# Two heads in one score product: half-zero query columns, loads by four heads, seven experts side by side

## The chip, the cores and the metric

The kernel runs on one core of a Trainium2 chip. The metric is the device time of one execution in microseconds (us), lower is better. Before the change it is 274.84 us, the median of three runs (272.33, 274.84 and 274.95).

The core has five engines that run their own queues of instructions: TensorE (PE, matrix products and transposes; PEld is its loading of stationary operands), VectorE (DVE), ScalarE (ACT), GpSimd (POOL) and SyncE (SP). Products are written to the memory PSUM, and DVE or ACT move them on to SBUF. POOL and SP also start DMA transfers.

## The reference

```python
def _attn_ref(q, k, v):                       # q, k, v: (8, 8, 576, 64)
    scores = np.matmul(q, k.transpose(0, 1, 3, 2)) / np.sqrt(64)
    rel = pos[:, None] - pos[None, :]
    scores = np.where((rel >= 0) & (rel < 64), scores, -1e9)
    ...softmax over the last axis...
    return np.matmul(attn, v)

def _moe_ref(x, phi, w1, w2):                 # x: (4608, 512), phi: (512, 32)
    logits = x @ phi
    d = softmax of logits over the tokens     # 8 experts x 4 slots = 32 columns
    slot_input = (d.T @ x).reshape(8, 4, 512)
    for e in range(8):                        # w1: (8, 512, 1024), w2: (8, 1024, 512)
        slot_out[e] = np.maximum(slot_input[e] @ w1[e], 0) @ w2[e]
    c = softmax of logits over the slots
    return c @ slot_out                       # (4608, 512)
```

First attention with a causal window of 64 keys, for 8 batches of 8 heads; its output, heads side by side, is x. Then a soft mixture of experts: 32 slots take a weighted mean over all tokens, each expert works on its four slots, and every token gets a weighted mean of the slots' results.

## The kernel before

**Stages.** First a loop over 32 pairs of heads (a batch has four pairs), staggered: in step n different pairs are in different stages. Then, once all batches are through, the slots' softmax is closed, the experts run, and the result is combined and written out (the last 63 us of the profile).

**A step n of the loop** issues in this order, as written out by hand (`manual_schedule`); each engine executes its own part in that order:

- `st_transpose` of pair n: 36 transposes of 64x64 blocks of q and k into tile tp (line 232).
- `st_score` of pair n-3: first ten products that write mask and maximum as a bias (`lh` with `rt`, lines 270 and 274), then 18 products of a block of 64 queries with 128 keys (lines 278 and 283). The two heads of a pair lie in partitions 0 to 63 and 64 to 127, so each product has 64 rows.
- `st_copy` of pair n: ACT brings the transposes of q and k to SBUF (line 235).
- `st_exp` of pair n-3: ACT, the exponentials of the scores (lines 291 and 292).
- `st_av` of pair n-4: 20 products of weights with values (lines 305 and 307). v1 holds v in blocks of 128 tokens, v2 the same shifted by 64.
- `st_shift` of pair n-2: transposes the maxima of the blocks of queries (line 258), DVE casts them into `rt` (line 262).
- `st_norm` of pair n-4: DVE divides by the sums and writes x_b (lines 316 and 317).
- `st_max` of pair n-1: two mask products of 480 columns (line 243), 36 products of 32 queries with 96 keys (line 250), and DVE's maximum over the keys (line 253).
- `fr_transpose` of pair n-5: five transposes of x (line 331), copied by ACT (line 332).
- Every fourth step one part of the mixture's softmax over tokens: logits (line 339, then DVE and the exponentials d of lines 355 to 358), dispatch (lines 386 to 392), the sums over tokens (lines 399 to 411).

The maximum that goes into the bias must not be below the largest score of a block, so scores are made twice: once for the maximum, once for the exponentials.

**Buffers.** The loop has four PSUM tiles of two banks that the names tp, sc, av, mx and f take in turn. Writes and reads of a tile are ordered by semaphores. `pin` holds two buffers each of q and k, a batch in each; POOL issues every load of q, k, v and weights (lines 76, 102, 104, 154), and copies v1 to v2 (lines 158 and 159).

**Experts.** Experts 0 to 3 run side by side: their products write 32 partitions each (lines 541 to 561). Experts 4 to 7 run one after another: 32 products of 4 columns (line 570), ReLU on ACT (line 573), eight products of 512 columns (line 578).

Of the kernel before, what the change touches and what calls it, by code (L numbers as in the profile page):

```python
# [18 lines left out]
def kernel(  # L19
# [33 lines left out]
    pin = ctx.enter_context(tc.tile_pool(name="pin", bufs=2))  # L53
# [5 lines left out]

    RQ = 9  # L60
    assert S == 64 * RQ

    def flat(src, b):
        return src[b].rearrange("h s d -> (h s) d").rearrange("(c p) d -> p c d", p=128)

    def rows(src, b):
        return src[b].rearrange("h s d -> (h s d)").rearrange("(g p x) -> p g x", p=128, x=RQ * Dh)

    staged = {}

    def new_qk(b):
        staged[b] = tuple(pin.tile([128, HP, RQ * Dh], FP16, name=n, tag=n) for n in ("qs", "ks"))

    def load_qk(b, c0=0, c1=HP):
        for t_, src in zip(staged[b], (q, k)):
            nc.gpsimd.dma_start(out=t_[:, c0:c1, :], in_=rows(src, b)[:, c0:c1, :])

    new_qk(0)
    load_qk(0, 0, 1)

    ident_h = const.tile([128, 128], FP16, name="ident_h")
    make_identity(nc, ident_h)
    load_qk(0, 1, HP)
# [22 lines left out]
    def load_last():  # L106
        e = E - 1
        w1_t[e], w2_t[e] = [], []
        for i in range(2):
            a = pin.tile([128, 2, F], FP16, name="w1h", tag="qs")  # L110
            nc.gpsimd.dma_start(out=a, in_=w1_dram(e)[:, 2 * i:2 * i + 2, :])
            w1_t[e].extend(a[:, j, :] for j in range(2))
        for i in range(2):
            c = pin.tile([128, 4, D], FP16, name="w2h", tag="ks")
            for j0, j1 in ((0, 4),) if i == 0 else ((0, 2), (2, 4)):
                nc.gpsimd.dma_start(out=c[:, j0:j1, :], in_=w2_dram(e)[:, 4 * i + j0:4 * i + j1, :])
            w2_t[e].extend(c[:, j, :] for j in range(4))


    wb = const.tile([32, 96], FP16, name="wb")  # L120
    nc.vector.memset(wb, 0.0)
    nc.gpsimd.affine_select(out=wb, in_=wb, compare_op=ALU.is_gt, fill=NEG,
                            base=0, pattern=[[1, 96]], channel_multiplier=-1)
    nc.gpsimd.affine_select(out=wb, in_=wb, compare_op=ALU.is_ge, fill=NEG,
                            base=64, pattern=[[-1, 96]], channel_multiplier=1)

    KR = 75
    mb = const.tile([64, 128], FP16, name="mb")
    nc.vector.memset(mb, 0.0)
    nc.gpsimd.affine_select(out=mb[:, 0:64], in_=mb[:, 0:64], compare_op=ALU.is_gt,  # L130
                            fill=NEG, base=0, pattern=[[1, 64]], channel_multiplier=-1)
    nc.gpsimd.affine_select(out=mb[:, 64:128], in_=mb[:, 64:128], compare_op=ALU.is_ge,
                            fill=NEG, base=0, pattern=[[-1, 64]], channel_multiplier=1)
    db = const.tile([128, 12], FP16, name="db")
    nc.vector.memset(db[64:128, :], 0.0)
    nc.gpsimd.affine_select(out=db[64:KR, 0:10], in_=db[64:KR, 0:10], compare_op=ALU.not_equal, fill=-1.0,
                            base=0, pattern=[[-1, 10]], channel_multiplier=1)
    nc.gpsimd.affine_select(out=db[64:KR, 10:11], in_=db[64:KR, 10:11], compare_op=ALU.not_equal, fill=NEG,
                            base=-10, pattern=[[0, 1]], channel_multiplier=1)
    nc.gpsimd.affine_select(out=db[64:KR, 11:12], in_=db[64:KR, 11:12], compare_op=ALU.not_equal, fill=1.0,  # L140
                            base=-10, pattern=[[0, 1]], channel_multiplier=1)
# [9 lines left out]
    v2s = [pvv.tile([128, NCH, VP], FP16, name=f"v2_{i}") for i in range(2)]  # L151

    def load_v(b):
        nc.gpsimd.dma_start(out=v1s[b % 2][:, :, 0:Dh], in_=flat(v, b))  # L154

    def shift_v(b):
        v1, v2 = v1s[b % 2], v2s[b % 2]
        nc.gpsimd.tensor_copy(out=v2[64:128, :, 0:Dh], in_=v1[0:64, :, 0:Dh])  # L158
        nc.gpsimd.tensor_copy(out=v2[0:64, 1:NCH, 0:Dh], in_=v1[64:128, 0:NCH - 1, 0:Dh])  # L159

    load_v(0)
    new_qk(1)
    load_qk(1)

    NQ = 4
    qkT = [pqk.tile([128, 2, 64 + S], FP16, name=f"qkT{i}") for i in range(NQ)]
    for t_ in qkT:
        nc.vector.memset(t_[:, 1, 0:64], 0.0)
    wm = const.tile([128, 5, 96], FP16, name="wm")
    for t in range(4):  # L170
        nc.vector.tensor_copy(out=wm[32 * t:32 * t + 32],
                              in_=wb[:, :].unsqueeze(1).broadcast_to([32, 5, 96]))
    nc.vector.memset(wm[0:32, 0, 0:64], NEG)
    nc.vector.memset(wm[32:64, 0, 0:32], NEG)

    lh = const.tile([128, 10, 128], FP16, name="lh")
    nc.vector.tensor_copy(out=lh[0:64], in_=mb[:, :].unsqueeze(1).broadcast_to([64, 10, 128]))
    nc.vector.tensor_copy(out=lh[64:128], in_=db[64:128, 0:10].unsqueeze(2).broadcast_to([64, 10, 128]))
    for u in (0, 5):
        nc.vector.tensor_tensor(out=lh[64:128, u, 0:64], in0=lh[64:128, u, 0:64],  # L180
                                in1=db[64:128, 10:11].broadcast_to([64, 64]), op=ALU.add)
    NR = 3
    rts = [const.tile([128, 128], FP16, name=f"rt{i}") for i in range(NR)]
    for rt in rts:
        nc.vector.memset(rt[64:128, 64:128], 0.0)
        nc.vector.tensor_copy(out=rt[64:128, 0:64], in_=db[64:128, 11:12].broadcast_to([64, 64]))
        nc.vector.tensor_copy(out=rt[0:64, 0:64], in_=ident_h[0:64, 0:64])
        nc.vector.tensor_copy(out=rt[0:64, 64:128], in_=ident_h[0:64, 0:64])
# [37 lines left out]
    def st_transpose(p, tq):  # L226
        b, hp = divmod(p, HP)
        for w, src in enumerate(staged[b]):
            for r in range(RQ):
                for hl in range(2):  # L230
                    h = slice(64 * hl, 64 * hl + 64)
                    nc.tensor.transpose(tq[h, w, 64 * r:64 * r + 64], src[h, hp, Dh * r:Dh * r + Dh], ident_h[h, h])  # L232

    def st_copy(p, tq):
        nc.scalar.activation(qkT[p % NQ][:, :, 64:64 + S].rearrange("p w (g r) -> p w g r", r=RQ),  # L235
                             tq[:, :, 0:S].rearrange("p w (r g) -> p w g r", r=RQ), AF.Copy, scale=QKS)

    def st_max(p):
        qk = qkT[p % NQ]
        m = pw.tile([128, 10], FP16, name="m", tag="m")  # L240
        mx, _ = banks("mx")
        for hl in range(2):
            nc.tensor.matmul(mx[:, hl, 0:480], ident_h[:, :], wm[:, :, :].rearrange("p c x -> p (c x)"),  # L243
                             start=True, stop=False, skip_group_check=True)
        for c in range(5):
            for t in range(4 if c < 4 else 2):
                o = 32 * (4 * c + t)
                for hl in range(2):
                    r = slice(64 * hl, 64 * hl + 64)
                    nc.tensor.matmul(mx[32 * t:32 * t + 32, hl, 96 * c:96 * c + 96],  # L250
                                     qk[r, 0, 64 + o:64 + o + 32], qk[r, 1, o:o + 96],
                                     start=False, stop=True, skip_group_check=True)
        nc.vector.reduce_max(m[:, :].rearrange("p (l c) -> p l c", l=2),  # L253
                             mx[:, :, 0:480].rearrange("p l (c x) -> p l c x", x=96), axis=AXX)
        mts[p] = m

    def st_shift(p, av):
        nc.tensor.matmul(av[64:74, 1, 384:512], mts.pop(p)[:, :], ident_h[:, :], start=True, stop=True,  # L258
                         skip_group_check=True)

    def st_shift_copy(p, av):
        nc.vector.tensor_copy(out=rts[p % NR][64:74, :], in_=av[64:74, 1, 384:512])  # L262

    def st_score(p, tp):
        qk, rt = qkT[p % NQ], rts[p % NR]
        pt = pw.tile([128, 2, 9, 64], FP16, name="pt", tag="pt")
        sc, _ = banks("sc")
        sm = tp[:, :, 288:352]
        for hl in range(2):
            nc.tensor.matmul(sm[:, hl, :], lh[:, 5 * hl + 4, :], rt[:, 0:64],  # L270
                             start=True, stop=False, skip_group_check=True)
        for hl in range(2):
            for c in range(4):
                nc.tensor.matmul(sc[:, hl, 128 * c:128 * c + 128], lh[:, 5 * hl + c, :], rt[:, :],  # L274
                                 start=(c == 0), stop=False, skip_group_check=True)
        for hl in range(2):
            r = slice(64 * hl, 64 * hl + 64)
            nc.tensor.matmul(sm[:, hl, :], qk[r, 1, 512:640], qk[r, 0, 576:640],  # L278
                             start=False, stop=True, skip_group_check=True)
# [30 lines left out]
    def st_norm(p, av):  # L310
        b, hp = divmod(p, HP)
        if hp == 0:
            xbs[b] = pxb.tile([128, 5, D], FP16, name="x_b", tag="x_b")
# [109 lines left out]
    for n in range(NP + 8):  # L423
# [7 lines left out]
        if ph == 3 and kb < B:  # L431
            shift_v(kb)
# [207 lines left out]
```

## Time and profile before

| | |
|---|---|
| time, median of 3 runs | 274.84 us |
| profiled execution: time | 271.76 us |
| its span, first to last instruction | 270.0 us |
| mean granted TensorE clock | 0.80 of full speed |
| steps 3 to 31 of the loop, scores' end to scores' end | 19.44 to 180.11 us |
| last slot product of the loop | 206.2 us |
| experts (line 541 to the copies so4) | 213.4 to 238.7 us |
| DMA, mean rate | 152 GB/s |

The profile is of one execution, somewhat below the median; sums are made against it. "Busy" is the share of time in which an engine executes an instruction. A busy TensorE need not run at its peak: products overlap, and its clock, which the profile gives as granted, is at times half. The chain of work that ended last can be followed back in this profile only to 207 us, so the loop is read from its timeline and from the waits.

### The profile page before, as it was taken

What the parts mean: (1) busy time and instruction counts of PE and PEld (TensorE: products, weight loads), DVE (VectorE), ACT (ScalarE), POOL (GpSimd) and SP (SyncE); (2) the same over time, 40 slices, a digit from 0 to 9 for tenths busy, and PEclk for the clock granted to TensorE, in tenths of its full rate; (3) what the DMA queues carried; (4) which work ended last, traced back from release to release, by engine and by line L of the source; (5) the groups of instructions that cost most, each with busy time, mean ns of one, the idle gap of its engine ahead of it and who ended that gap; (6) DMA issues with size and microseconds to landing.
All of it is one profiled execution on the core that took longest, in us unless ns stands there. A gap on an engine that the chain in (4) does not pass through costs nothing. (4 is left out here: it accounts for less than half of the span.)

```text
span 270.0 us, 9905 instructions
## 1 busy us (share of the span) xinstructions
PE 185.6 (69%) x4563; PEld 122.6 (45%) x4563; DVE 140.9 (52%) x313; ACT 120.5 (45%) x215; POOL 78.0 (29%) x74
## 2 busy tenths in 40 slices
PE   2386858858868897887887586878663488866400
PEld 1254646646646665665665365555531134521100
DVE  2743563674754576674485554656664621056510
ACT  2235445655455475574654647462632111155400
POOL 8566064342370533443057033740000000000000
PEclk9998989986985897997799689975955557995555
DMA  6999997992999599199299959899960000029996
GB/s 84 175 206 210 181 208 131 177 207 38 132 211 208 58 187 206 17 177 208 37 100 210 210 73 184 121 203 205 210 105 0 0 4 0 2 101 344 359 359 234
DMA packets 63625, 41.06 MB, mean 152 GB/s; under 512 B 38496, under 2 KB 54880, under 8 KB 63584
## 3 DMA queue, kind: packets, MB, share of 16 engines
q0 software_dynamic: 58064, 30.94, 84.3%
q1 hardware_dynamic: 5520, 9.50, 10.2%
q8 instruction: 35, 0.57, 0.8%
q14 instruction: 6, 0.05, 0.1%
HBM read 61.93 MB, written 9.44 MB: 264 GB/s over the span
## 5 line engine op out<-in xcount | busy, mean ns | idle before, releaser
L235 ACT ACTIVATE qkT<-tp 128x1152 f16<-128x1152 f16 x32 | 36.2, 1131 | 50.2 <-PE tp L278 39.6
L253 DVE TENSOR_REDUCE m<-mx 128x10 f16<-128x960 f32 x32 | 36.8, 1150 | 6.4 <-PE mx L250 6.2
L262 DVE CAST rt<-av 10x128 f16<-10x128 f32 x32 | 9.2, 289 | 51.6 <-PE av L258 50.9
L292 ACT ACTIVATE pt<-sc 128x1024 f16<-128x1024 f32 x32 | 32.9, 1029 | 0.6 <-PE sc L283 0.5
L332 ACT COPY xt<-f 128x576 f16<-128x576 f16 x32 | 20.5, 640 | 26.5 <-PE f L331 26.5
L154 POOL DMA_DIRECT2D v<-in_v_dram x8 | 14.6, 1823 | 55.3 <-issue 35.2
L158 POOL COPY v<-v 64x2304 f16<-64x2304 f16 x8 | 16.8, 2102 | 41.6 <-DMA v<-in_v_dram 41.6
L317 DVE TENSOR_TENSOR x_b<-av,rc 128x640 f16<-128x640 f32 x32 | 26.4, 824 | 1.1
L305 PE MATMUL av<-v,pt 128*64 128x65 f16 x576 | 19.7, 214 | 8.0 <-issue 8.0
L232 PE MATMUL tp<-ident_h,qs 64*64 64x64 f16 x576 | 17.6, 210 | 11.0 <-DMA qs<-in_q_dram 7.9
L274 PE MATMUL sc<-rt,lh 128*128 128x128 f16 x256 | 23.9, 247 | 1.4 <-issue 1.4
L243 PE MATMUL mx<-wm,ident_h 128*128 128x480 f16 x64 | 21.7, 426 | 3.0 <-ACT pt L291 2.7
L305 PEld LDWEIGHTS <-pt 128*64 128x64 f16 x576 | 15.3, 125 | 12.2 <-issue 8.6
L232 PEld LDWEIGHTS <-qs 64*64 64x64 f16 x576 | 14.2, 122 | 14.4 <-DMA qs<-in_q_dram 8.0
L232 PE MATMUL tp<-ident_h,ks 64*64 64x64 f16 x576 | 17.6, 210 | 4.6 <-issue 2.4
L250 PEld LDWEIGHTS <-qkT 64*32 64x32 f16 x1152 | 11.3, 97 | 18.5 <-issue 18.3
L274 PEld LDWEIGHTS <-lh 128*128 128x128 f16 x256 | 18.4, 113 | 1.6 <-issue 1.6
L283 PE MATMUL sc<-qkT 64*128 64x64 f16 x512 | 15.8, 205 | 4.4 <-issue 4.4
L331 PE MATMUL f<-ident_h,x_b 128*128 128x128 f16 x160 | 16.3, 240 | 2.5 <-ACT pt L291 1.2
L250 PE MATMUL mx<-qkT 64*32 64x96 f16 x1152 | 16.2, 221 | 2.2 <-issue 2.2
L232 PEld LDWEIGHTS <-ks 64*64 64x64 f16 x576 | 14.6, 125 | 5.1 <-DMA ks<-in_k_dram 2.6
L159 POOL COPY v<-v 64x2240 f16<-64x2240 f16 x8 | 16.4, 2052 | 0.5
(135 smaller groups left out, 295.0 us busy)
## 6 DMA issues: line engine op xcount, KB each, us to landing
w<-in_moe_w_dram POOLq DMA_DIRECT2D x14, 1024.0 KB, 15.6
out_dram<-ob SPq DMA_DIRECT2D x16, 512.0 KB, 4.5
v<-in_v_dram POOLq DMA_DIRECT2D x8, 576.0 KB, 8.4
qs<-in_q_dram POOLq DMA_DIRECT2D x7, 576.0 KB, 9.6
ks<-in_k_dram POOLq DMA_DIRECT2D x7, 576.0 KB, 11.6
w1h<-in_moe_w_dram POOLq DMA_DIRECT2D x2, 512.0 KB, 18.6
out_dram<-ob SPq DMA_DIRECT2D x8, 128.0 KB, 4.5
w2h<-in_moe_w_dram POOLq DMA_DIRECT2D x1, 512.0 KB, 19.1
```

Of the source, the lines that this page charges most:

```text
L158: nc.gpsimd.tensor_copy(out=v2[64:128, :, 0:Dh], in_=v1[0:64, :, 0:Dh])
L159: nc.gpsimd.tensor_copy(out=v2[0:64, 1:NCH, 0:Dh], in_=v1[64:128, 0:NCH - 1, 0:Dh])
L232: nc.tensor.transpose(tq[h, w, 64 * r:64 * r + 64], src[h, hp, Dh * r:Dh * r + Dh], ident_h[h, h])
L235: nc.scalar.activation(qkT[p % NQ][:, :, 64:64 + S].rearrange("p w (g r) -> p w g r", r=RQ), tq[:, :, 0:S].rearrange("p w (r g) -> p w g r ...
L243: nc.tensor.matmul(mx[:, hl, 0:480], ident_h[:, :], wm[:, :, :].rearrange("p c x -> p (c x)"), start=True, stop=False, skip_group_check=True)
L250: nc.tensor.matmul(mx[32 * t:32 * t + 32, hl, 96 * c:96 * c + 96], qk[r, 0, 64 + o:64 + o + 32], qk[r, 1, o:o + 96], start=False, stop=Tru ...
L253: nc.vector.reduce_max(m[:, :].rearrange("p (l c) -> p l c", l=2), mx[:, :, 0:480].rearrange("p l (c x) -> p l c x", x=96), axis=AXX)
L274: nc.tensor.matmul(sc[:, hl, 128 * c:128 * c + 128], lh[:, 5 * hl + c, :], rt[:, :], start=(c == 0), stop=False, skip_group_check=True)
L292: nc.scalar.activation(pt[:, :, 0:8, :].rearrange("p l i x -> p l (i x)"), sc[:, :, :], AF.Exp, scale=XS)
L305: nc.tensor.matmul(av[r0:r0 + 64, hl, 65 * (i // 2):65 * (i // 2) + 65], pt[:, hl, i, :], rhs, start=True, stop=True, skip_group_check=True)
L317: nc.vector.tensor_tensor(out=xbs[b][:, :, 128 * hp:128 * hp + 128].rearrange("p c (l d) -> p l c d", l=2), in0=avv[:, :, :, 0:64], in1=rc ...
L332: nc.scalar.copy(out=xts[b][:, hp, :], in_=fq[:, 0, 0:S])
```

## The change

In the loop the two heads of a score product now stand in one product of 128 rows. Four heads are loaded together (`load_rows`: a "quad", a step of two loads of 288 KB for k and q, one for v). Even steps transpose k of a quad, odd steps q. After the transpose the partitions hold 64 dimensions of head h and 64 of head h+2; q goes into `qbs`, where each block has 64 columns for the first head with zeros in the lower partitions and 64 columns for the second with zeros in the upper ones. One product of 128x128 then gives the scores of both heads.

- `st_transpose`: 18 transposes a step instead of 36, of 128 rows. `st_copy`: one activation for k, two for q.
- `st_max` of pair n-2 in place of n-1: 3 mask products and 9 products of 128x128 instead of 2 and 36; the ninth block's place is in tile tp (`m8`), and DVE's maximum is split in two.
- `st_shift` moves to pair n-3, in the same step as its score, and writes to tile tp instead of av.
- `st_score`: 9 bias and 9 score products instead of 10 and 18; its ninth block's place is in av instead of tp.
- The order in a step: transposes, copy, shift with its cast, maximum, scores with exponentials, values, normalising.
- `fr_transpose`: ten transposes and one copy every second step instead of five and one every step.
- Loads of q, k and v by quads, four buffers; v2 is shifted by quads; v is loaded two steps earlier. The weights' loads stand at steps 0, 3, 6 to 30.
- Experts 4, 5 and 6 run side by side as a second group; only expert 7 goes by itself.

```diff
-    pin = ctx.enter_context(tc.tile_pool(name="pin", bufs=2))
+    pin = ctx.enter_context(tc.tile_pool(name="pin", bufs=4))
...
+    def load_rows(src, g, tag):
+        t = pin.tile([128, 2, RQ * Dh], FP16, name=tag, tag=tag)
+        b, gq = divmod(g, 2)
+        nc.gpsimd.dma_start(out=t, in_=src[b].rearrange("h s d -> (h s d)").rearrange(
+            "(g p x) -> p g x", p=128, x=RQ * Dh)[:, 2 * gq:2 * gq + 2, :])
+        staged[tag, g] = t
...
+    def load_v(g):
+        b, gq = divmod(g, 2)
+        c = slice(NVC * gq, NVC * gq + NVC)
+        nc.gpsimd.dma_start(out=v1s[b % 2][:, c, 0:Dh],
+                            in_=v[b].rearrange("h s d -> (h s) d").rearrange("(c p) d -> p c d", p=128)[:, c, :])
...
+    def st_transpose(n, tq):
+        g, odd = divmod(n, 2)
+        src = staged.pop(("qs" if odd else "ks", g))
+        tf = tq.rearrange("p a x -> p (a x)")
+        for r in range(RQ):
+            for hf in range(2):
+                nc.tensor.transpose(tf[64 * hf:64 * hf + 64, 128 * r:128 * r + 128],
+                                    src[:, hf, Dh * r:Dh * r + Dh], ident_h[:, :])
+
+    def st_copy(n, tq):
+        g, odd = divmod(n, 2)
+        tf = tq.rearrange("p a x -> p (a x)")[:, 0:2 * S].rearrange("p (r l g) -> p l g r", r=RQ, l=2)
+        if odd:
+            for hf in range(2):
+                h = slice(64 * hf, 64 * hf + 64)
+                nc.scalar.activation(qbs[g % 2][h, :, :, hf, :], tf[h], AF.Copy, scale=QKS)
+        else:
+            nc.scalar.activation(kTs[g % NK][:, :, 64:64 + S], tf, AF.Copy, scale=QKS)
...
+    def at(two, one, i):
+        return two[:, i // 4, 128 * (i % 4):128 * (i % 4) + 128] if i < 8 else one
...
+        m8 = tp[:, 1, 256:384]
+        nc.tensor.matmul(m8, ident_h[:, :], wm[:, 1, :], start=True, stop=False, skip_group_check=True)
+        for j in range(2):
+            nc.tensor.matmul(mx[:, j, :], ident_h[:, :], wm[:, j:j + 4, :].rearrange("p c x -> p (c x)"),
                              start=True, stop=False, skip_group_check=True)
...
+        for i in [8] + list(range(8)):
+            nc.tensor.matmul(at(mx, m8, i), qblock(p, i), kwindow(p, i), start=False, stop=True,
+                             skip_group_check=True)
+        nc.vector.reduce_max(m[:, 8:9], m8, axis=AXX)
...
+        nc.tensor.matmul(tp[64:64 + NB, 1, 128:256], mts.pop(p)[:, 0:NB], ident_h[:, :], start=True, stop=True,
                          skip_group_check=True)
...
+        nc.vector.tensor_copy(out=rts[p % NR][64:64 + NB, :], in_=tp[64:64 + NB, 1, 128:256])
...
+        sm = av[:, 0, 384:512]
+        order = [8] + list(range(8))
+        for i in order:
+            nc.tensor.matmul(at(sc, sm, i), lh[:, i, :], rt[:, :], start=(i % 4 == 0), stop=False,
+                             skip_group_check=True)
+        for i in order:
+            nc.tensor.matmul(at(sc, sm, i), kwindow(p, i), qblock(p, i), start=False, stop=True,
+                             skip_group_check=True)
...
         if n < NP:
             st_transpose(n, tq)
+            st_copy(n, tq)
         if 0 <= n - 3 < NP:
-            sc, sm = st_score(n - 3, tp)
...
+            st_shift(n - 3, tp)
+        if 0 <= n - 2 < NP:
+            st_max(n - 2, tp)
+        if 0 <= n - 3 < NP or 0 <= n - 4 < NP:
             av, _ = banks("av")
+        if 0 <= n - 3 < NP:
+            st_score(n - 3, av)
         if 0 <= n - 4 < NP:
             st_av(n - 4, av)
...
+    groups = ((0, 1, 2, 3), (4, 5, 6))
...
+    for g, es in enumerate(groups):
+        ha, _ = banks("ha")
+        n = 32 * len(es)
+        for f2 in range(2):
+            for kk in range(NKK):
+                for j, e in enumerate(es):
+                    nc.tensor.matmul(ha[32 * j:32 * j + 32, f2, :], sit[:, kk, :],
+                                     w1_t[e][kk][:, 512 * f2:512 * f2 + 512],
+                                     start=(kk == 0), stop=(kk == NKK - 1), skip_group_check=True)
```

## The prediction

> **What bounds the kernel now.** I read the page first. No engine is full: TensorE (PE) is busy 69% of the span. The granted clock changes between full and half; and the program's own instructions come by DMA in 35 packets (0.57 MB, so 16 KB each; PE's 2 x 4563 rows are about 260 a packet).
>
> ```profile
> PE 185.6 (69%) x4563; PEld 122.6 (45%) x4563; DVE 140.9 (52%) x313; ACT 120.5 (45%) x215; POOL 78.0 (29%) x74
> ...
> PEclk9998989986985897997799689975955557995555
> ...
> q8 instruction: 35, 0.57, 0.8%
> ```
>
> Then the timeline of one undisturbed step of the loop (start, duration, instruction; the bracket is idle time and what ended it). The step before began its transposes at 113.67 and this one at 117.48, as soon as the large exponential had ended: 3.81 us a step, made of transposes, bias and score products (1.5 us of PE) and then on ScalarE (ACT) the copy of the transposes, 1.13, and two exponentials, 0.27 and 1.03. While ACT copies, PE does weighted values, shift and maximum products: they belong to other pairs and wait for nothing new.
>
> ```profile
> 116.40 1.03 ACT L292 ACTIVATE pt<-sc 128x1024 f16<-128x1024 f32 x1
> 117.48 0.47 PE L232 MATMUL tp<-ident_h,qs 64*64 64x64 f16 x18 [0.19 <-ACT pt L292]
> ...
> 118.24 0.61 PE L274 MATMUL sc<-rt,lh 128*128 128x128 f16 x8
> 118.82 0.40 PE L283 MATMUL sc<-qkT 64*128 64x64 f16 x16
> 119.03 1.13 ACT L235 ACTIVATE qkT<-tp 128x1152 f16<-128x1152 f16 x1 [1.05 <-PE tp L278]
> 119.58 0.22 PE L258 MATMUL av<-ident_h,m 128*10 128x128 f16 x1
> 119.84 0.29 DVE L262 CAST rt<-av 10x128 f16<-10x128 f32 x1 [1.35 <-PE av L258]
> 120.21 1.03 ACT L292 ACTIVATE pt<-sc 128x1024 f16<-128x1024 f32 x1
> 120.25 0.47 PE L250 MATMUL mx<-qkT 64*32 64x96 f16 x36
> ```
>
> The list of waits (total, times, longest) says two more things. L399 writes one bank of tile f while ACT reads the other, and still waits: a wait goes by whole tile. And PE stands at "issue", with nothing of the program in the way, every 256 rows or so: 14 such gaps of 0.8 to 2.7 us between 20 and 180 us, 24 us in all, each near one of the instruction packets.
>
> ```profile
> ACT qkT L235 <- PE tp L278: 39.6, 24, 3.3
> PE av L305 <- issue: 8.0, 5, 2.7
> PE f L399 <- ACT xt L332: 5.1, 7, 0.7
> ```
>
> Last, busy time in windows as long as the clock's stretches (multiples of 3.41 us). 57% busy at full clock was followed by full clock, 51% by half; half ended only after a window with PE busy throughout.
>
> ```profile
> 164.63:168.04 3.41, 1.95 (x78) 1.67 (x76) 0.89 (x1) 2.36 (x4) 1.69 (x1) 1.00 1.49 204
> 168.04:171.45 3.41, 2.62 (x98) 1.79 (x99) 2.08 (x4) 0.57 (x2) 3.35 (x4) 1.00 0.81 153
> 174.87:178.29 3.42, 1.74 (x53) 1.42 (x50) 2.85 (x6) 2.85 (x7) 0.17 (x1) 1.00 1.18 194
> 178.29:181.70 3.41, 3.06 (x49) 1.79 (x46) 0.60 (x3) 2.21 (x3) 2.70 (x4) 0.50 1.15 211
> ```
>
> The score products of step 3 end at 19.44 and those of step 31 at 180.11: 28 steps of 5.74 us, the 3.81 plus instruction gaps, half clock and the softmax over slots that comes every fourth step. That is 161 of 270 us and where the change acts.
>
> **What it does to a step.** PE's order in the changed program is: 18 transposes, shift, 1+2 mask products, 9 maximum products, 9 bias, 9 scores, 20 weighted values, then transposes of x (10, every second step). Tile tp is now written by the transposes, read by the copy, written by the shift, read by VectorE's (DVE) cast, and written by the maximum's ninth block. So by the whole-tile rule PE stops after the transposes until the copy ends, stops again for the cast, and all the products that the copy used to cover stand behind these two waits. The built program has both waits. The copy in turn queues on ACT behind the large exponential of the step before. The loop becomes one chain, each link from a row above, hops of 0.05 included:
> - after the last score (S): exponential 1.08;
> - even steps: copy of x, now 128x1152 once in two steps. It has the size of L235, 1.13, less 0.1 of overlap; PE's transposes end first (S+0.95);
> - copy of transposes: k in one of 1.13; q in two, each on 64 partitions, each with all 1152 elements a partition. No such row is shown. ACT took 266 ns for 128x128 and 178 for 64x32, 0.9 ns an element whatever the partitions, so 2 x 1.13, overlapped 2.2. (If half the partitions cost half: 1.1, and 15 us less in the whole; I keep that for the lower end.)
> - shift to end of cast: 119.58 to 120.13, 0.6 with hops;
> - products to the new S: 0.06 + 2 x 0.21 (L243, 0.2 for 480 columns) + 27 at 57 ns (L274: 8 in 0.61, of which 0.2 is latency) + 0.2 = 2.2.
>
> Even to odd: 1.08+1.02+2.2+0.6+2.2 = 7.1. Odd to even: 1.08+1.13+0.05+0.6+2.2 = 5.05. Two steps 12.15, against 7.6 for two undisturbed ones now. Weighted values (0.5), transposes (0.7: 128x64 tiles in two column halves like L305; one by one like L274 it would be 1.2, of which 0.3 would show in even steps) and the maximum's reduce (1.22 for 1024 elements by L253) lie beside the exponential and cost nothing; were that cover gone, transposes and values would add 1.2 a step.
>
> Every fourth step adds the slots' work in the same queues. Logits: the d exponentials wait for DVE (normalise to S+1.4, then 1.5 of reductions) and take 1.2; the next copy is behind them: +3.0. Dispatch: +1.2 (PE waits for the copy of x, then two copies and an exponential on ACT). Accumulation: +0.95 (slot products, and DVE's combine ahead of the cast). From step 3 to 31: 14 x 12.15 = 170, and 6 x 3.0 + 6 x 1.2 + 5 x 0.95 = 30. **200 us against 161: +39**, at full clock.
>
> **Clock.** Of 7 us PE is busy some 4.1 (0.7+0.2+2.2+0.5+0.3+0.2), 57%, and the idle part is in one piece of 1.2 to 4 us before the long run of products. The window that holds it falls under the 51-57% seen above, so the products start at half clock, until a window lies inside the run. They have 2.0 us of streaming, which half clock doubles: 0 to 2.0 more a step. I take 0.6 of it, since the run (at half: 4.2 plus values, transposes) holds one full window and often regains full clock at its end: 1.2 x 28 = **+33**.
>
> **Fewer products.** 74 a pair instead of 128, but not less PE time: 16 L283 take 0.2 us beside latency, the nine that replace them 0.5; 36 L250 take 0.25, their nine 0.5. By the Trainium skill ("TensorE: Matmul & The Clock Gate", section Back-to-back issue gap) starts lie at least 25 ns apart however small the product, and 54 fewer would save 1.35 us a step, 43 us in all. The trace disagrees: 36 in 0.47 us, 7 ns apart. What does go is instruction gaps: 5534 PE rows for 9118, and 256 rows now last about 12 us where the packets came every 5 to 6. The chain was summed without them; were all 13 left, +20.
>
> **Loads and v.** Loads of 288 KB start earlier and smaller; PE waited for q and k only in the first 12 us (8 us). Step 3's scores come about 3 us earlier (maxima after the second k, near 10.5): **-3**. The tenth value product reads chunk 0 of v1, which the load for two batches later is now writing in step 4b-2: that load is issued when the previous step's values end and is needed a step (8 us) later. 576 KB landed in 8.4 us, 144 KB in 3.3: 0, bounded by 6 x 1.5 = 9. It holds POOL's queue, where k, q, weights and shifts stand with several steps to spare. Constants: beside the first loads.
>
> **Drain and experts.** After the last score the lags (9, 10, 11) are the same: 26 us now, +-1 either way; I add 1. Experts: from 213.4 to 238.7 now. Three of four rounds of L570/L573/L578 go (3.05 each, 9.2, and 1.2 of L578 at half clock). Added: two more halves of L541 (1.9 each at half clock, less some), 24 more of L557 (1.7 to 2.4). 10.4-3.6-2 = 4.8, and the copy osb is halved over two engines and partly covered: **-6** (-3 to -8).
>
> **Sum.** Profiled execution 271.76 (span 270.0): +39+33-3+1-6 = 336. The median of the runs shown is 274.84, 1.1% above it: 339.
>
> **Rivals.**
> - *The chain at full clock.* If only a stretch without any product slowed the clock, no idle piece here (up to 4 us, never a whole window) would, and the second term is 0: 303, or 306 on the median. Against it: 174.87, halved at 51% busy. The Trainium skill says this ("TensorE: Matmul & The Clock Gate", Part 1 and the table at its end): an idle window of about 3.4 us throttles, gaps under 3 us do not. The trace has half clock after windows that were half busy. 15%.
> - *Half clock nearly always:* 2.0 plus 0.4 for transposes that then delay the copy, x 28 = 67: 370, 374 on the median. For it: 178.29 stayed half at 3.06 of 3.41 busy. 13%.
> - *Faster: PE's feed is the bound.* If the copy and cast wait is covered after all, the 24 us of instruction gaps go and -3-6 stay: 271.8-33 = 239. It decides where the new serial part costs under 24/28 = 0.86 us a step. Against: copy plus cast alone are 1.7 to 2.8, and the tile wait is in the rows of L399. 5%.
> - *Partly covered* (q copies cheaper, extras hidden): 275 to 300, 5%.
>
> **Numbers.** Main case 62%: 339, its own range 315 to 362. Range 300 to 365: it takes in the full-clock case and leaves out the faster ones and most of the always-half one. 1% is what a measurement tells from no change: faster 0.05, same 0.01, slower 0.94.
>
> **What would show it.** The shift's line waiting on ACT's copy 1 us or more in nearly every step; the ninth block's line on DVE's cast; transposes 5 to 9 us apart, long after even steps; q's copy twice 1.13; PEclk near 0.7 in the loop; "issue" gone from PE. Wrong if PE does not idle between transposes and shift, or if steps stay under 6 us.

## The result, and the profile after

The changed kernel takes 359.32 us (median of four runs, 357.96 to 360.36); the kernel before takes 273.58 (median of four, 269.22 to 274.95). The ratio is 1.327, with a 95% interval of 1.312 to 1.342: 86 us slower. The profiled execution after took 360.36 us, its span is 358.6 against 270.0. Some executions of a kernel run over 1.5% longer than its fastest, and one of e1_untie took 761.6 us with TensorE slow from end to end: the medians below are over all executions but that one, the ratios and their intervals without any of the slow ones.

The page of the kernel after, in the rows that were shown of the one before, and one group of instructions:

```profile
PE 215.3 (60%) x2771; PEld 159.9 (45%) x2771; DVE 155.9 (43%) x341; ACT 142.4 (40%) x214; POOL 96.4 (27%) x113
...
PEclk9999869866886679886788666668987885579555
...
q8 instruction: 21, 0.34, 0.4%
...
L248 ACT ACTIVATE qb<-tp 64x1152 f16<-64x1152 f16 x32 | 36.0, 1125 | 4.9 <-PE tp L239 4.5
```

PE has 1792 products fewer and is nevertheless busy 30 us longer; more of its time is at half clock (mean granted clock 0.767 against 0.799). 14 of the 35 instruction packets are gone. The copy of q on 64 partitions takes 1125 ns, as long as the old one on 128 (1131).

The timeline shows what a step has become. In the row of 174.66 the bracket says that PE sat idle for 2.74 us and that ACT's copy ended it.

```profile
171.22 0.69 PE L239 MATMUL tp<-ident_h,qs 128*64 128x128 f16 x18
171.33 1.12 ACT L339 COPY xt<-f 128x1152 f16<-128x1152 f16 x1 [0.68 <-PE f L337]
...
172.35 2.26 ACT L248 ACTIVATE qb<-tp 64x1152 f16<-64x1152 f16 x2
174.66 0.27 PE L278 MATMUL tp<-ident_h,m 128*9 128x128 f16 x1 [2.74 <-ACT qb L248]
...
174.96 0.29 DVE L280 CAST rt<-tp 9x128 f16<-9x128 f32 x1 [3.48 <-PE tp L278]
175.30 0.26 PE L265 MATMUL tp<-wm,ident_h 128*128 128x128 f16 x1 [0.38 <-DVE rt L280]
...
176.32 1.06 PE L270 MATMUL mx<-kT,qb 128*128 128x128 f16 x8
...
177.28 0.86 PE L289 MATMUL sc<-rt,lh 128*128 128x128 f16 x8
...
178.04 0.61 PE L292 MATMUL sc<-qb,kT 128*128 128x128 f16 x8
...
178.30 0.28 ACT L294 ACTIVATE pt<-av 128x128 f16<-128x128 f32 x1 [3.69 <-PE av L292]
```

The engines take turns: transposes, copy of x, copy of q, shift, cast, then 30 products, of which the first eight of L270 take 1.06 us at half clock and the eight of L292 0.61 at full; ACT meanwhile has nothing to do for 3.69 us. Before, the copy had products of other pairs beside it.

The list of waits (total, times, longest) has the same three links over the whole execution:

```profile
PE tp L278 <- ACT qb L248: 38.1, 15, 2.7
...
PE tp L278 <- ACT kT L250: 31.7, 14, 4.0
...
PE tp L265 <- DVE rt L280: 18.3, 31, 2.7
```

Together PE stands 88 us behind the copy and the cast, two waits that the kernel before did not have. PE's own waits for "issue", 22 us in 17 pieces before, are gone from the list.

Where the 88.6 us of span are:

| stretch | before | after | difference |
|---|---|---|---|
| up to the scores of step 3 | 19.4 | 22.4 | +2.9 |
| steps 3 to 31, scores' end to scores' end | 160.7 | 251.2 | +90.5 |
| from there to the last slot product | 26.1 | 30.3 | +4.2 |
| to the first expert product | 7.2 | 7.2 | 0 |
| experts, to the copies so4 | 25.3 | 17.0 | -8.3 |
| combine and write out | 31.3 | 30.5 | -0.8 |

### The profile page after: what moved, and what is told of

It is laid out like the page before. It is cut to its first block, busy times and chain, and to the rows that moved or that the text cites. A ratio compares the mean times of both kernels' runs of the same rounds, so it can differ in the third digit from the quotient of the medians.

```text
span 358.6 us, 6470 instructions
## 1 busy us (share of the span) xinstructions
PE 215.3 (60%) x2771; PEld 159.9 (45%) x2771; DVE 155.9 (43%) x341; ACT 142.4 (40%) x214; POOL 96.4 (27%) x113
## 5 line engine op out<-in xcount | busy, mean ns | idle before, releaser
L273 DVE TENSOR_REDUCE m<-mx 128x8 f16<-128x1024 f32 x32 | 39.2, 1225 | 15.4 <-PE mx L270 15.2
L248 ACT ACTIVATE qb<-tp 64x1152 f16<-64x1152 f16 x32 | 36.0, 1125 | 4.9 <-PE tp L239 4.5
L270 PEld LDWEIGHTS <-qb 128*128 128x128 f16 x288 | 30.5, 139 | 14.8 <-issue 12.7
L270 PE MATMUL mx<-kT,qb 128*128 128x128 f16 x256 | 31.2, 295 | 0.0
L292 PE MATMUL sc<-qb,kT 128*128 128x128 f16 x256 | 29.5, 284 | 0.0
L267 PE MATMUL mx<-wm,ident_h 128*128 128x512 f16 x64 | 29.4, 556 | 0.0
L292 PEld LDWEIGHTS <-kT 128*128 128x128 f16 x288 | 28.2, 136 | 0.0
L71 POOL DMA_DIRECT2D qs<-in_q_dram x16 | 11.4, 712 | 52.2 <-PE tp L239 51.5
L321 DVE RECIPROCAL rc<-av 128x10 f32<-128x10 f32 x32 | 7.1, 221 | 39.4 <-PE av L311 39.4
L250 ACT ACTIVATE kT<-tp 128x1152 f16<-128x1152 f16 x16 | 18.1, 1131 | 9.9 <-PE tp L239 9.6
L339 ACT COPY xt<-f 128x1152 f16<-128x1152 f16 x16 | 17.9, 1119 | 10.0 <-PE f L337 9.0
```

Source lines behind the costliest of these rows:

```text
L248: nc.scalar.activation(qbs[g % 2][h, :, :, hf, :], tf[h], AF.Copy, scale=QKS)
L250: nc.scalar.activation(kTs[g % NK][:, :, 64:64 + S], tf, AF.Copy, scale=QKS)
L267: nc.tensor.matmul(mx[:, j, :], ident_h[:, :], wm[:, j:j + 4, :].rearrange("p c x -> p (c x)"), start=True, stop=False, skip_group_check=True)
L270: nc.tensor.matmul(at(mx, m8, i), qblock(p, i), kwindow(p, i), start=False, stop=True, skip_group_check=True)
L273: nc.vector.reduce_max(m[:, 0:8].rearrange("p (l c) -> p l c", l=2), mx[:, :, :].rearrange("p l (c x) -> p l c x", x=128), axis=AXX)
L292: nc.tensor.matmul(at(sc, sm, i), kwindow(p, i), qblock(p, i), start=False, stop=True, skip_group_check=True)
```

## The experiments

Theory: the change turned the loop into one chain, because by the whole-tile rule shift and maxima, and with them everything behind them in PE's queue, wait for the copy of the same step (the tile tie); the idle piece that this makes drops the clock. Rivals: the wide products or the longer copies are themselves the loss; the clock is lost for another reason; loads are late.

**Untying the tiles.** In e1b_shift the shift alone leaves tile tp, for tile f, and goes ahead of the transposes; in e1_untie and e1_again the ninth block of the maxima also leaves tp, for av.

```diff
-    def st_shift(p, tp):
-        nc.tensor.matmul(tp[64:64 + NB, 1, 128:256], ...
+    def st_shift(p, f, bank):
+        nc.tensor.matmul(f[64:64 + NB, bank, 384:512], ...
...
-        m8 = tp[:, 1, 256:384]
+        m8 = av[:, 1, 384:512]          # e1_untie, e1_again
...
+            st_shift(n - 3, f, 0 if sb is not None else 1)
             st_transpose(n, tq)
             st_copy(n, tq)
-            st_shift(n - 3, tp)
```

> The changed kernel with the shift alone moved to tile f; the maximum's ninth block stays in tile tp behind the copy. Chain theory: the copy still stands in the chain, only shift and cast (20.9 us in 28 steps, 0.6 to 1.9 each) go out of it: 17 to 21 us less, 338 to 343. Rival, the two waits are one and the same and the copy alone decides: no change, 356 to 361. Rival, the shift was the tie that mattered: as fast as with both moved, below 300.

> The changed kernel with the shift moved to tile f and the maximum's ninth block to tile av, so that nothing behind the transposes on TensorE waits for ScalarE's copy of the same step; all products, copies and exponentials stay. Chain theory: the step is then set by ScalarE (7.1 us in two steps and about 1 us a step of the slots' work) or by TensorE alone (about 4.4 us at full clock), 4.8 to 5.8 us a step instead of 8.97, so 28 steps give 89 to 117 us back: 242 to 270 us, and TensorE no longer idles between transposes and mask products. Rival, the wide products themselves at half clock are the cost (3.6 us of products, 0.5 of values, 0.7 of transposes and 0.7 of the rest a step): 6 us a step or more, 275 to 300. Rival, ScalarE's longer copies are the cost whatever TensorE waits for: above 330.

> The changed kernel with the shift in tile f and the ninth block of the maxima in tile av, so that nothing behind the transposes waits for their copy: the kernel of e1_untie once more, to see what bounds it, since the profiled execution of the first was not like the timed ones. Its timed median was 295, 6.6 us a step from 295-359 = -64 us in 28 steps against 8.97. Theory 1, the clock: PE works 5 us a step at mixed clock and the products (27 of 128 columns before the scores, 9+9 after) run at half rate in most steps; then products that come in eights take 0.9 to 1.1 us, and the granted clock is near 0.8. Theory 2, a wait that took the place of the removed one: PE idles before one line in nearly every step, by 1 us or more, for ACT or DVE; then the list of waits has one pair with 28 or more times and over 28 us in all. Time 293 to 297 by both.

e1b_shift: 337.54 us, just under the chain's 338 to 343. e1_untie: 293.63, ratio to before 1.091 (1.081 to 1.101): 64 us of the 86 come from two tile addresses and one line's place. That is not the 242 to 270 that the chain theory hoped for; the number lies in the range of the rival by which wide products at half clock are the cost.

e1_again, the same kernel (299.88 us, 293.68 to 301.20; the profiled execution is the fastest), shows what bounds the rest, and it is not that rival: the eight scores take 0.61 us, which is full clock, in 26 of 32 steps, where the changed kernel has 8 of 32. Of the two theories for e1_again neither holds alone: undisturbed steps take 5.4 to 5.5 us, and no wait of PE comes 28 times. Two rows of its list of waits matter:

```profile
PE av L312 <- DMA v<-in_v_dram: 16.0, 3, 14.5
...
PE sc L290 <- ACT qb L248: 11.2, 12, 1.1
```

In the second the biases of the scores, which write tile sc and read nothing of the copy, wait for ACT to have read tp. Five names take four places, and by this wait sc now gets the place of this step's own tp. The copy has left the maxima's way and stands in that of the scores. The first row is another matter, taken up below.

**The other direction: the old kernel with a tie.** e5_btie changes nothing but the tile that the shift of the kernel before writes.

```diff
-        nc.tensor.matmul(av[64:74, 1, 384:512], mts.pop(p)[:, :], ident_h[:, :], ...
+        nc.tensor.matmul(tp[64:74, 1, 384:512], mts.pop(p)[:, :], ident_h[:, :], ...
```

> The kernel before with one line's tile exchanged: the transposed maxima (line 258) go to tile tp, in a part that nobody else writes, instead of tile av. By the whole-tile rule the shift now waits until ACT has copied the transposes out of tp and has taken its small exponential from it, and all products behind it on PE (mask, maxima, transposes of x) wait too; the products ahead of it (weighted values) still cover part of the copy. Theory of the tile tie: the shift starts about 0.8 us later in a step, so do the maxima, and the step of 5.74 us grows by 0.5 to 0.8 us: +15 to +22 us in 28 steps, 285 to 295 in all, and the trace has PE waiting for ACT at line 258 in nearly every step. Rival, by which the tie costs nothing where the kernel's old order is kept, because the next step's transposes wait for the large exponential anyway: 0 to +5 us, 270 to 276. Rival, by which hardware orders by address and not by tile: no wait of PE for ACT at line 258 at all, 0.

285.53 us against 271.91, ratio 1.043 (1.034 to 1.051), 9 to 14 us where 15 to 22 was expected. The wait is there, and the sign; an undisturbed step has grown from 3.81 to 4.34 us. Nobody else writes these columns of tp, so in this program it is the tile and not the address that is waited for:

```profile
PE tp L258 <- ACT pt L291: 20.4, 23, 2.5
```

**The clock.** e3_fill gives PE products that nobody reads in the place where it waits for the copy, and leaves the chain as it is.

```diff
+            for _ in range((12, 24, 32, 20)[n % 4]):
+                nc.tensor.matmul(av[:, 0, 384:512], ident_h[:, :], lh[:, 1, :], start=True, stop=True, ...
             st_shift(n - 3, tp)
```

> The changed kernel with 12, 24, 32 or 20 extra products of 128x128 that nobody reads, placed where TensorE waits for the copy (steps 4 to 31). They take no place in the chain, but keep the array at work. Clock theory (half clock follows from idle stretches and costs 39 us of the 101 us that the products from cast to last score take): products 2.2 to 2.7 us a step instead of 3.6, 25 to 40 us less: 320 to 334, granted clock above 0.85. Rival, the clock does not follow the idle time: granted clock 0.77 as before, 358 to 370 since the extra products can only delay.

331.54 us, ratio 1.227 (1.219 to 1.235): 616 products more, and 28 us less. The page's row of granted clock, against that of the changed kernel above:

```profile
PEclk9979969999997999997979799999998555587555
```

The links of the chain, summed over 28 steps from the timelines, show where that went:

| link (us in 28 steps) | after | e3_fill |
|---|---|---|
| scores' end to start of the copy | 81.4 | 83.2 |
| copy | 47.5 | 47.5 |
| copy's end to cast's end | 20.9 | 21.3 |
| cast's end to scores' end | 101.3 | 66.3 |
| of the last, at half clock | 81.4 | 9.8 |

Only the last link has changed, and it has lost the time at half clock. Idle pieces between products cost the clock, as the theory has it, and in the profiled executions they cost 35 us.

**A shorter copy.** e2_qdve has DVE copy the second half of q.

```diff
-            for hf in range(2):
-                h = slice(64 * hf, 64 * hf + 64)
-                nc.scalar.activation(qbs[g % 2][h, :, :, hf, :], tf[h], AF.Copy, scale=QKS)
+            nc.scalar.activation(qbs[g % 2][0:64, :, :, 0, :], tf[0:64], AF.Copy, scale=QKS)
+            nc.vector.tensor_scalar(out=qbs[g % 2][64:128, :, :, 1, :], in0=tf[64:128], scalar1=QKS, ...
```

> The changed kernel with the second half of q's copy on VectorE beside the first on ScalarE. Chain theory: odd steps' copy is 1.2 instead of 2.26 us, 14 x 1.05 = 15 us less at the same clock, and up to 6 more because TensorE idles less: 338 to 346. Rival, the copy is covered by other work: within 2 us of 359.

367.99 us, slower than the changed kernel: a miss. From its timeline:

```profile
171.29 1.12 ACT L246 ACTIVATE qb<-tp 64x1152 f16<-64x1152 f16 x1
172.45 1.36 DVE L247 TENSOR_SCALAR qb<-tp 64x1152 f16<-64x1152 f16 x1 [2.12 <-ACT qb L246]
173.86 0.27 PE L278 MATMUL tp<-ident_h,m 128*9 128x128 f16 x1 [3.00 <-DVE qb L247]
```

DVE did not copy beside ACT but after it, although both only read tp and write different partitions of qb: in the built program the one waits for the other. So the link got longer and not shorter: 2.52 us for 2.26 in an odd step, 51.4 for 47.5 in 28 steps.

That this sets the time is not shown by this run. Its span has grown by 3.4 us (362.0 for 358.6), about as much as the longer copies, but also as much as a wait of PE for v that has nothing to do with the copy, and the products took 95.5 us for 101.3. The row of this wait, in the changed kernel and then in e2_qdve:

```profile
PE av L311 <- DMA v<-in_v_dram: 2.3, 1, 2.3
```

```profile
PE av L311 <- DMA v<-in_v_dram: 5.8, 1, 5.8
```

The median is 8.7 us above that of the changed kernel; what makes the rest of it stays open.

**The products without the new order.** e6_order keeps the change's products, loads and experts, and puts a step back in the old order, with a pair scored one step later.

```diff
             st_transpose(n, tq)
-            st_copy(n, tq)
-            st_shift(n - 3, tp)
-            st_max(n - 2, tp)
-            st_score(n - 3, av)
-            st_av(n - 4, av)
-            st_norm(n - 4, av)
+            sc, sm = st_score(n - 4, tp)    # the ninth block's score straight behind its bias
+            ...                             # k's copy, the exponentials, q's copy
+            st_av(n - 5, av)
+            st_shift(n - 3, av)
+            st_norm(n - 5, av)
+            st_max(n - 2, av)               # the ninth block last
```

> The changed kernel with its products, loads and experts, but in the order of the kernel before: transposes, scores, exponentials, weighted values, shift, normalising, maxima; k's copy stands ahead of the exponentials, q's behind them; the shift goes to tile av as before, the ninth block of the scores to tp, of the maxima to av. Pairs are scored one step later, so the loop has one step more, and v is loaded one step later. Nothing on PE stands behind the copy of its own step but the maxima and the next transposes. Theory, that the order and the tiles made the loss: even step 0.9 of transposes, 0.3, copy 1.13, exponentials 1.3; the odd step 0.9, scores 1.1, exponentials 1.3, and its copy of 2.26 runs into the next even step; with the copy of x 9.3 for two steps, 4.65 each against 3.81 undisturbed before: 0.84 x 28 = +23, experts -8, one step more and the start +1: about 288, 275 to 300. Rival, that the wide products and the longer copies themselves make the loss (the scores, maxima and values at half clock, ACT 1.7 a step for copies): over 320.

290.13 us against 272.41, ratio 1.066 (1.059 to 1.073). The number is the theory's, but that is luck, since it is made otherwise. Undisturbed steps take 4.5 and 5.1 us, near the 4.65 worked out; on top of that stand 40.1 us in which PE waits for v, which the 288 did not have in it. The longest of these waits, in e6_order's timeline:

```profile
28.62 0.34 PE L316 MATMUL av<-v,pt 128*64 128x65 f16 x9
51.20 0.21 PE L318 MATMUL av<-v,pt 128*64 128x65 f16 x1 [22.24 <-DMA v<-in_v_dram]
```

L318 is the tenth product of values. It reads chunk 0 of v1 into rows that nobody uses, and in every second quad the load that POOL has issued in the same step is writing that chunk.

**One index.** e8_order_v is e6_order, and e9_v the changed kernel, with the tenth product reading a chunk of its own quad.

```diff
-                             pt[:, 8, 64 * hf:64 * hf + 64], v1[:, 0, 0:65], ...
+                             pt[:, 8, 64 * hf:64 * hf + 64], v1[:, NVC * gq, 0:65], ...
```

> e6_order with one index changed: the tenth product of weighted values, whose rows nobody uses, reads the first chunk of its own quad of v1 instead of chunk 0, which in every second quad the load for two batches later is just writing. In e6_order PE waited 40.1 us for that load, 6 times, 22.2 the longest (values of quad 1, 28.96 to 51.20, behind 9 MB of loads). Theory, that only this read ties the values to the load: no wait of that line is left, and the time falls by 22 to 40: 250 to 268, at or below the 264.5 of the kernel before with the changed experts. Rival, that the loads themselves are late (the DMA engines are full until 50 us) and another line will wait for k, q or v instead: -5 at most, 285 to 290.

> The changed kernel with that one index changed and nothing else. The prediction priced this wait at 0 with a bound of 9; the profile of the changed kernel has 2.3 us of it, once. Theory, that the slow chain leaves the load its time: 0 to -2, ratio to the changed kernel within 1%, 355 to 361. Rival, that a wait shown under other lines (POOL's queue held, exponentials late) hides more of it: -5 to -9, 350 to 354.

e8_order_v: 261.82 us against 270.66, ratio 0.966 (0.958 to 0.974), and no wait for v at that line. The index cost 28 us there, and the loop without it takes 157.1 us from the scores of pair 0 to those of pair 28, no more than the 160.7 before, where e6_order's theory had 23 us more.

In the changed kernel the index cost more than the 2.3 us that the list of waits had: e9_v takes 351.74, ratio to before 1.299 (1.292 to 1.307) against 1.327 (1.312 to 1.342), some 7 us. The spans differ by 7.4, 6.9 of it before 90 us: 2.0 in the step with the wait (8.23 to 6.21), 2.1 in the next (8.57 to 6.48), whose products had run at half clock and now do not; another 2.1 are in a step ahead of the wait, which the index can't explain, and 1 in the steps behind.

So the rival's number came true; some 4 of its 7 us fit the wait and the clock that it took with it, as far as two single executions can show it.

**The experts alone.** e4_tail is the kernel before with the changed kernel's experts.

> The kernel before with one part of the change alone: the experts as the changed kernel runs them (0 to 3, then 4 to 6 side by side, then 7). The loop is untouched. In the changed kernel the stretch from the first expert product to the copies so4 took 17.05 us against 25.3 before, and the stretch after it 30.4 against 31.3. If that gain belongs to the experts' part and not to what the changed loop leaves behind (an idle PE, other weights' arrival), this kernel is 8 us faster than the one before, 6 to 9: ratio about 0.97. The prediction had 6 for it (3 to 8). Rival: the changed kernel reached its experts 100 us later, with all weights long in place; here the weights of experts 4 to 7 may land only just in time, and the gain is 0 to 3 us, ratio 0.99 to 1.0, with PE waiting for DMA in the products of experts 4 to 6.

264.49 us against 271.91, ratio 0.970 (0.964 to 0.976). First expert product to the copies so4: 215.5 to 233.8, 18.4 us for 25.3. The weights are there in time.

**Two more changes of order.** The first is given in outline. e7_small_first is e4_tail with the ninth block's score products of the kernel before straight behind their bias; e10_norm_last is e8_order_v with the normalising behind the maxima.

```diff
# e7_small_first, st_score
         sm: biases (2)
-        sc: biases (8)
         sm: products (2)
+        sc: biases (8)
         sc: products (16)
# e10_norm_last, the step
-            st_norm(n - 5, av)
             st_max(n - 2, av)
+            st_norm(n - 5, av)
```

> The kernel before with the experts of the changed one (e4_tail), and one more edit: in the scores the ninth block's products with k and q come straight behind its bias, ahead of the other biases and scores. They write tile tp, for which ACT's copy waits, so the copy can start about 0.5 us earlier in a step (in the step from 117.48 to 121.3 it waited 1.05 us, until 119.03, for a product that began at 118.78, behind 0.61 of biases). Theory A, the chain through ACT alone sets the step: 0.5 x 28 = -14 at most, -10 to -14 against e4_tail: 251 to 255 where the kernel before takes 272. Theory B, PE is next: its own work of a step is about 3.6 of the 3.81 us (0.69 transposes, 1.1 scores, 0.5 values, 0.45 shift and masks, 0.45 maxima, 0.4 transposes of x), so 0.2 x 28 = -6 at most, 0 to -6: 259 to 265. B is the likelier.

> e8_order_v with one exchange of order: the normalising of pair n-5 stands behind the maxima of pair n-2, not ahead of them. In e8_order_v PE waited 21.8 us in 27 steps (0.8 each) with the ninth block of the maxima, which writes tile av, for DVE to have read av in the normalising; PE is otherwise busy 4.0 of the 4.8 us of an undisturbed step. Theory, that by the whole-tile rule this wait goes and PE, the bound, gets a part of it back: 0.4 to 0.8 x 28, -11 to -22 from 262: 240 to 251. Rival, that the later normalising holds av, whose place a later tile of the ring takes, so that another line of PE waits for the same DVE instruction: 0 to -3, 259 to 262, or slower by up to 0.8 x 28 = 22.

Neither moved the time: 265.78 (ratio 0.979, 0.973 to 0.984) beside e4_tail's 264.49, and 261.59 (0.968, 0.961 to 0.974) beside 261.82.

In e7_small_first ACT waits less for tp (25.2 us for the 39.6 before), and an undisturbed step is 3.77 us for 3.81. But ACT's wait for the transposes of x has grown from 26.5 to 42.4 us. So theory A falls, and of theory B's 0 to -6 nothing came; that PE is next fits this, but no run shows it.

In e10_norm_last the wait for the normalising is gone. In e8_order_v it was:

```profile
PE av L271 <- DVE x_b L329: 21.8, 27, 2.1
```

Counted from transposes to transposes, undisturbed steps that transpose k fell from 4.51 to 3.86 us, and those that transpose q rose from 5.06 to 5.27. In the lists of waits some 19 of the 21.8 us are back at other lines: 6.6 at the same block for DVE's cast, 4.7 more for ACT's copy of x, 3.2 more for ACT's exponentials d, and 4.3 at the transposes and the score biases. So the gain was handed on to other tiles, as the rival has it, though not by the DVE instruction that it named.

So two kernels, with the variants just shown, beat both: the old loop with the new experts (0.970), and the new products in the old order with one index mended (0.966); their intervals overlap, and no run compared them directly.

## Why the prediction was right

The forecast was 339 of 300 to 365, by the chain with its two waits at partly half clock; 359.32 came. The mechanism is what the timeline, the list of waits, e1b_shift, e1_untie, e5_btie and e3_fill show. On the profiled execution the sum was 336, and 360.4 came, near the upper end of the main case's 315 to 362: all larger misses but the experts' lie on one side. By terms, the extras put where they fall:

| term | predicted | measured |
|---|---|---|
| scores' end to copy | 69.7 | 81.4 |
| copies (14 of 1.13, 14 of 2.2) | 46.6 | 47.5 |
| copy's end to cast's end, with the combines | 21.6 | 20.9 |
| products, full clock 61.6 and clock 33 | 94.6 | 101.3 |
| start | -3 | +2.9 |
| drain | +1 | +4.2 |
| experts and the rest | -6 | -9.1 |

- **Copies.** Right to 1 us. The doubt whether half the partitions cost half is settled by the row of L248: elements per partition count.
- **Scores' end to copy** was 12 us too small. By steps modulo 4 from 0: 1.08, 2.1, 3.65 and 3.13 were worked out, 1.73, 2.27, 3.82 and 3.82 measured. The accumulation makes 4.3 of it (0.86 more ahead of the copy in each of its five steps), the dispatch 2.2 (1.2 was taken, 1.6 came), the logits 1.1. Another 2.6 stand in one step without slot work, step 7, behind the wait for v, so they belong to the term of v; the other steps without slot work miss by 1.4 together. Full clock makes this link little shorter: without step 7 it has 73.5 us in e3_fill for 76.7, so it is made of waits more than of slow products.
- **Clock.** Right in kind. 33 was taken between 0 and 56; the products took 39.4 more than at their full-clock 2.21 a step. That the size came near is in part luck: the share of 51 to 57% busy by which it was judged does not hold in the profile after (see the last section). The rival of the full clock falls: of the clock's windows between 20 and 275 us none is wholly idle (the lowest is 6% busy), half clock began 23 times in the loop where PE stood idle for over 3 us only six times, and filling the idle pieces gave 35 us of the products back. The Trainium skill ("TensorE: Matmul & The Clock Gate", Part 1) has half clock come after an idle window of about 3.4 us; in these traces it also comes without one. The rival of half clock nearly always was nearer than its 13%: 81.4 of the 101.3 us ran at half, and at half throughout they would have been 113.4. Its 374 us were not reached.
- **Start.** The sign was wrong: step 3's scores end at 22.4 us and not at 16.4. The first maxima begin at 12.2 and not at 10.5, and the products of the first two steps that have any run at half rate (eight of L270 in 1.06 us), about 3 us more; the rest is not taken apart.
- **Drain.** 3 us too small. The chain goes on after step 31: from its scores to those of step 34 it takes 18.3 us for 12.7 before, which the +1 did not have.
- **v.** "0, bounded by 9" was the step that failed in its kind: the wait was seen, and dismissed because the load has a step's time. The list of waits has 2.3 us of it; without the read the kernel is 7 us shorter, of which at least 4 fit it, and in faster loops the same read cost up to 28 us.
- **Fewer products, PE's feed.** The gaps went with the packets, as said (35 to 21), and so did PE's 22 us of "issue". That can show only where the chain is gone: in e8_order_v undisturbed steps are about 1 us longer than before, and yet the loop is not.
- **Experts.** -8.3 for -6; the second group's halves cost less than taken (12 products in 1.04 us in the last half, at full clock by then).

What the prediction did not say is that the products themselves are no loss: e8_order_v, with them, is level with e4_tail, without them. It priced the change as a whole, and the loss lay in the order of a step and in which name takes which place.

## What to carry to other kernels

When an edit merges work, look first at which tiles the new order makes two engines share within one step: a write that waits for a copy of the same step stops everything behind it in that engine's queue, and it cost far more here (64 us by two tile addresses and one line's place) than the 22 us of waits for instructions that the merging took away. Untying one name hands the wait to the next one as long as more names than places go round, so follow the ring of places until an engine, and not a place, is the bound. Idle time that a new wait makes is paid twice where it also takes the clock, and a read whose result nobody uses is still a wait.

## What the runs showed of the hardware

The clock does not go by PE's busy share alone. These windows of the changed kernel (stretch, length, then busy time and count of PE, PE's loads, DVE, ACT and POOL, granted clock, DMA, GB/s) are as long as the clock's stretches:

```profile
136.83:140.24 3.41, 1.62 (x21) 1.26 (x21) 0.80 (x3) 1.35 (x2) 0.00 (x0) 1.00 0.66 87
140.24:143.65 3.41, 2.31 (x68) 1.92 (x66) 2.98 (x7) 1.30 (x2) 1.63 (x2) 1.00 0.00 0
...
198.28:201.70 3.42, 2.06 (x46) 1.30 (x45) 2.61 (x6) 2.15 (x2) 2.50 (x3) 1.00 0.16 11
201.70:205.11 3.41, 1.82 (x12) 1.26 (x12) 1.77 (x4) 0.00 (x0) 1.77 (x2) 0.50 1.74 175
```

A window with PE busy for 1.62 us was followed by full clock, one with 2.06 by half. The first holds wide products (21 rows), the second many small ones (46), so what is counted may be the work in the array; no run tested that. And at the start products took twice their time (eight in 1.06 us, up to about 30 us) while the record of granted clock still says 1.0; its first change stands at 34.4 us.
